# Ten staging places, another start order and a new sharing of ScalarE, VectorE and GpSimd in a fused attention and two feed-forward layers

## The chip, the cores and the metric

The kernel runs on one core of a Trainium2 chip. The metric is the device time of one execution in microseconds, as the median of the runs shown. Lower is better.

## The reference

For each of 8 batches and 8 heads, 512 tokens `x` (64 wide) attend to 32 state rows and the state rows attend to the tokens. Both results stand one behind the other as 544 rows of 512 numbers per batch (4352 rows in all). They go through a feed-forward layer with a leaky ReLU (512 to 2048 to 512) and then through a gated one (512 to 1536 to 512).

```python
scores = scale * np.matmul(x, state.transpose(0, 1, 3, 2))
a = softmax(scores);  xread = np.matmul(a, state)
scores2 = scale * np.matmul(state, x.transpose(0, 1, 3, 2))
a2 = softmax(scores2);  sread = np.matmul(a2, x)
x = concatenate([xread, sread], axis=2)     # then heads side by side
h = x @ w_in;  x = np.maximum(0.01 * h, h) @ w_out
g = x @ w_gate
out = g * sigmoid(g) * (x @ w_val) @ w_out2
```

The weights are float64 in the inputs. The kernel gets their bits as pairs of 32-bit words and rounds them to float32 itself.

## The kernel before

**Products.** A float32 operand is split into a high and a low part (`split_h` on ScalarE, line 164, `split_l` on VectorE, line 167), and a product is three TensorE passes over these parts. The first layer doesn't form `xread`: since `xread @ w_in` is `a @ (state @ w_in)`, the kernel multiplies the state by `w_in` once for all batches and then works with the softmax `a` (parts `ah`, `al`) and the product (parts `swh`, `swl`).

**The product of state and w_in.** `product_sw` (line 462) makes it for a group of 512 columns `g`, a pair of heads `p` and four batches `bs`: two matmuls, one for each head, into two PSUM banks (`ps_sw`). Both banks are copied to staging tiles `sw` (line 476) and each is stored to `sw_dram` by a transfer that SyncE issues (line 477). Head 0 of a pair has two staging tiles (pool `cv`), head 1 two others (pool `xin`), four in all. There are 32 such products, so 64 copies and 64 stores. `load_sw` (line 491) fetches a batch's rows back when that batch's turn comes. Batch 0 needs its part at once: `state_win` makes it by itself (line 456), and `keep_sw_h`, `keep_sw_l` split it out of PSUM.

**Conversion of a weight tile.** There are 32 tiles of 128 x 512 in the first layer, 16 of `w_in` and 16 of `w_out` (order: `ORDER`, line 90). A tile is loaded as `ws` (512 KB, five places), and `to_f32` (line 208) has six steps for it: `scale` (L214) and `low` (L215) on ScalarE; `sign` (L216), `limit` (L219), `join` (L222) and `add` (L225) on VectorE. `limit` caps the scaled high word, `add` adds the rounding bits of the low word to the joined word. The generator `convert` (line 234) runs them as a pipeline of four pumps to a tile: `scale` of this tile and `limit` of the one before; `low` and `sign` of this tile; `join` of the one before; `add` of the one before, with the next load, and, for `w_in`, a store to `win_dram` (L232). `w_out` tiles are then split into high and low parts (`w_parts`).

**What sets the order.** Instructions stand on each engine in the order in which the program issues them, and an engine takes them in that order. Two kinds of strings, written by hand, set it in the first stage. `START` (line 91) is walked once: `c` is one pump of the conversion, `p` one product, `0` and `1` the next step of the scores and the softmax of the first batch's two halves, `h` and `l` the high and low part of batch 0's own product, `s` and `S` the placing of the state of batch 0 and of the other batches in `states` (`place_states`, line 1223), `m` the first product with `ah`, `al` (`h_mm`, line 510). `SLOT0` (line 92) has one string for each of the 16 slots of batch 0: `c` and `p` as above, `H` the next `h_mm`, `S` and `L` its splits (`gh`, `gl`), `Y` and `Z` the halves of `y_mm`, the product with `w_out`. In `START` a product takes two of the four banks of pool `ps_y`; in `SLOT0` it takes the two single banks of `ps_a`, which the next product must find emptied. The later batches and the second layer follow, with orders of their own.

## Time and profile before

| | |
|---|---|
| median of three runs | 1471.0 us (1470.5, 1471.0, 1475.11) |
| the profiled execution's own time | 1474.11 us |
| its span, first to last instruction | 1471.8 us |
| TensorE matmuls (PE) | 1444.4 us busy, 98% of the span |
| VectorE (DVE) | 829.1 us, 56% |
| ScalarE (ACT) | 688.0 us, 47% |
| GpSimd (POOL) | 3.0 us, 8 instructions |
| DMA | 309.65 MB, mean 210 GB/s |

Busy shares are means over stages that differ. The page's 40 slices show TensorE at nine tenths or more in all slices but the first and the last. VectorE and ScalarE are busiest in the first four slices, the first 150 us, and so are the DMA engines. The chain of work that ended last is 95% TensorE. The stage to read is therefore the first one, by windows, waits and timelines.

### The profile page before, as it was taken

The page shows a single profiled execution, that of the slowest core. Times are in us where ns is not written, and L with a number is a line of the kernel's source. Part 1 is how long each engine was busy: PE and PEld are TensorE (multiplying, and loading weights), DVE is VectorE, ACT ScalarE, POOL GpSimd, SP SyncE. Part 2 cuts the span into 40 slices and gives each one's busy share as a digit, 9 for nine tenths or more (in the row PEclk, how much of TensorE's full clock was granted, in tenths as well). Part 3 has the DMA queues.
Part 4 walks back from the last instruction along what each step waited for, and adds up shares of the span by engine and source line. Part 5 has one row for each costly group of instructions (what it writes and reads, how often), then busy time and mean ns, then how long its engine had stood idle before and what let it go on. Part 6 is the DMA issues. An engine that isn't in the chain of part 4 may idle for free.

```text
span 1471.8 us, 20667 instructions
## 1 busy us (share of the span) xinstructions
PE 1444.4 (98%) x7530; PEld 1153.9 (78%) x7530; DVE 829.1 (56%) x1476; ACT 688.0 (47%) x1243; POOL 3.0 (0%) x8
## 2 busy tenths in 40 slices
PE   5999999999999999999999999999999999999998
PEld 1545777777777778888888888888888878988887
DVE  5877577676767676243454535555344655544442
ACT  6877556555656666444333433334233343333322
POOL 0000000000000000000000000000000000000000
PEclk9999999999999999999999999999999999999999
DMA  8996556665665656260668666667766397876345
GB/s 293 321 327 216 184 183 241 199 225 193 220 217 184 237 183 210 99 206 23 211 194 279 228 231 208 193 218 244 232 194 194 102 319 238 270 247 193 117 152 191
DMA packets 146788, 309.65 MB, mean 210 GB/s; under 512 B 14080, under 2 KB 34816, under 8 KB 145664
## 3 DMA queue, kind: packets, MB, share of 16 engines
q1 hardware_dynamic: 145392, 299.82, 61.8%
q10 hardware_dynamic: 1296, 8.52, 1.4%
q8 instruction: 60, 0.98, 0.3%
q14 instruction: 40, 0.33, 0.1%
HBM read 231.74 MB, written 76.55 MB: 209 GB/s over the span
## 4 chain that ended last, share of the span: by engine, by line
PE 95%; DMA 2%; ACT 1%; DVE 1%; issue 0%; SPq 0%; ACTq 0%
PE ps_y L444 24%; PE ps_o L444 18%; PE ps_x L729 18%; PE ps_h L444 14%; PE ps_s L729 9%; PE ps_a L729 4%; PE ps_t L444 2%; PE ps_sw L468 2%; PE ps_yt L444 2%; PE ps_s L319 1%; DMA sw_dram<-sw 1%; PE ps_r L416 1%; ACT sw L476 1%; DMA wo<-wo 1%; PE ps_a L402 0%
## 5 line engine op out<-in xcount | busy, mean ns | idle before, releaser
L444 PE MATMUL ps_y<-gh,w_parts 128*128 128x512 f32 x1024 | 340.5, 392 | 0.0
L729 PE MATMUL ps_x<-yc,wq 128*128 128x512 f32 x1152 | 278.1, 389 | 0.0
L729 PEld LDWEIGHTS ps_x<-yc,wq 128*128 128x128 f32 x1152 | 216.2, 188 | 44.9
L444 PE MATMUL ps_o<-wo,zh 128*128 128x512 f32 x768 | 236.4, 389 | 0.0
L444 PEld LDWEIGHTS ps_y<-gh,w_parts 128*128 128x128 f32 x1024 | 193.0, 188 | 52.1 <-issue 7.6
L444 PE MATMUL ps_y<-gl,w_parts 128*128 128x512 f32 x512 | 200.0, 391 | 0.0
L168 DVE TENSOR_TENSOR gl<-hs,gh 128x512 fp32r<-128x512 f32 (+1 forms) x144 | 95.1, 660 | 142.8 <-ACT gh L165 142.6
L444 PEld LDWEIGHTS ps_o<-wo,zh 128*128 128x128 f32 x768 | 144.1, 188 | 29.9
L537 ACT ACTIVATE hs<-ps_h 128x512 f32<-128x512 f32 (+1 forms) x144 | 82.6, 574 | 171.9 <-PE ps_h L444 168.2
L444 PE MATMUL ps_o<-wo,zl 128*128 128x512 f32 x384 | 149.5, 389 | 0.9 <-DMA wo<-wo 0.9
L729 PE MATMUL ps_s<-yc,wq 128*128 128x512 f32 x576 | 146.2, 389 | 0.0
L168 DVE TENSOR_TENSOR zl<-z,zh 128x512 fp32r<-128x512 f32 x96 | 66.3, 691 | 115.7 <-ACT zh L165 115.6
L729 PEld LDWEIGHTS ps_s<-yc,wq 128*128 128x128 f32 x576 | 108.1, 188 | 22.5
L165 ACT CAST zh<-z 128x512 fp32r<-128x512 f32 x96 | 59.3, 622 | 141.6 <-PE ps_o L444 141.5
L749 ACT ACTIVATE sg<-C 128x512 f32<-128x512 f32 x72 | 45.5, 632 | 158.2 <-DVE C L745 158.2
L444 PEld LDWEIGHTS ps_y<-gl,w_parts 128*128 128x128 f32 x512 | 96.6, 189 | 19.7
L444 PE MATMUL ps_h<-ah,swl 128*128 128x512 f32 x256 | 106.4, 416 | 1.1 <-DVE swl L168 1.1
L745 DVE TENSOR_TENSOR C<-ps_s,C 128x512 f32<-128x512 f32 x48 | 33.2, 691 | 123.0 <-PE ps_s L729 122.9
L444 PE MATMUL ps_h<-al,swh 128*128 128x512 f32 x256 | 100.4, 392 | 0.5 <-DVE al L168 0.5
L741 ACT COPY C<-ps_x 128x512 f32<-128x512 f32 x96 | 55.9, 583 | 94.7 <-PE ps_x L729 93.2
L444 PE MATMUL ps_h<-ah,swh 128*128 128x512 f32 x256 | 100.1, 391 | 0.0
L165 ACT CAST gh<-hs 128x512 fp32r<-128x512 f32 (+1 forms) x144 | 85.6, 595 | 3.0
(129 smaller groups left out, 1910.3 us busy)
## 6 DMA issues: line engine op xcount, KB each, us to landing
wo<-wo SPq DMA_DIRECT2D x96, 512.0 KB
wq<-quad_gate SPq DMA_DIRECT2D x168, 256.0 KB
wq<-quad_val SPq DMA_DIRECT2D x168, 256.0 KB
ws<-in_dram SPq DMA_DIRECT2D x68, 512.0 KB
sw_dram<-sw SPq DMA_DIRECT2D x64, 256.0 KB
sw<-sw_dram SPq DMA_DIRECT2D x56, 256.0 KB
quad_gate<-hl SPq DMA_DIRECT2D x24, 512.0 KB
quad_val<-hl SPq DMA_DIRECT2D x24, 512.0 KB
```

What stands on the lines that cost most here:

```text
L165: nc.scalar.copy(dst, src)
L168: nc.vector.tensor_tensor(out=dst, in0=src, in1=hi.bitcast(F32), op=ALU.subtract)
L319: nc.tensor.matmul(ps[2 * NS * i:2 * NS * (i + 1)], lhsT=states[:, p, b, :], rhs=xt.pop((b, p)), start=True, stop=True,)
L416: nc.tensor.matmul(ps[NS * k:NS * (k + 1), i], lhsT=v["et"][:, n:n + NS], rhs=tokens[i][:, c, NS * k:NS * (k + 1)], start=(c == 0), stop=( ...
L444: nc.tensor.matmul(ps, lhsT=w, rhs=v, start=first and n == 0, stop=last and n == len(todo) - 1)
L468: nc.tensor.matmul(ps[e], lhsT=flat[half, p, 4 * bs:4 * bs + 4, :].rearrange("d b n -> d (b n)"), rhs=raw["in", g, p][half], start=True, s ...
L476: nc.scalar.copy(t, ps[e])
L537: nc.scalar.activation(hs, ps[:, :n], AF.Prelu, alpha=0.01)
L729: nc.tensor.matmul(bank, lhsT=a, rhs=v, start=first and n == 0, stop=last and n == len(todo) - 1, skip_group_check=True,)
L741: nc.scalar.copy(t[0], src)
L745: nc.vector.tensor_tensor(out=kept[0], in0=bank, in1=kept[0], op=ALU.add)
L749: nc.scalar.activation(t[0], c, AF.Sigmoid)
```

## The change

Line numbers behind the change are those of the new file, up to 19 higher.

- The state product is staged in ten tiles, five for each head of a pair, which are taken in turn (`stage_sw`). Six of them are parts of tiles that are first used later (`yst`, `x_tail`).
- ScalarE copies the first bank of a product, VectorE the second. Of the products of batches 0 to 3 only rows 32 to 127 are stored, without batch 0's rows.
- `limit` and `add` of a first-layer tile run on GpSimd, but for the first four tiles. `add` is there an integer `tensor_tensor`. There are 28 such tiles, 56 instructions. The tiles of the second layer stay on VectorE.
- The state of batches 1 to 7 is placed by GpSimd (two copies). Batch 0's stays on ScalarE.
- ScalarE runs one copy of a 128 x 1 tile before anything else.
- `START` is another string. `SLOT0` is unchanged.

```diff
--- before.py
+++ after.py
@@ -88,7 +88,7 @@
 
     LOADS = "xswxxwww"
     ORDER = "iiiioiiooiioiioioiioioioiooooooo"
-    START = "spc0Scpccc0p0cpccpcc1ccchcc1cccpc1clcpp0hcccpclp1c01cpcmcc"
+    START = "sccccScc0ccpc0cpccp1c0cpcchc1cpcc0lp1hc0cpccpl1cpcp1cpcmcc"
     SLOT0 = [
         "DcHcpAccccSYLpcZccc",
         "DcHcAcccpSYLpccZccc",
@@ -210,19 +210,21 @@
         lo, low3 = t.bitcast(U32)[:, :, 0], t[:, :, 0]
         hi, hi_f = t[:, :, 1], t.bitcast(F32)[:, :, 1]
         v = raw[key].bitcast(I32)
+
+        engine = nc.gpsimd if key[0] in ("in", "out") and key not in keys1[:4] else nc.vector
         return {
             "scale": lambda: nc.scalar.activation(hi_f, hi_f, AF.Copy, scale=REBIAS),
             "low": lambda: nc.scalar.activation(low3, lo, AF.Copy, scale=2.0 ** -29),
             "sign": lambda: nc.vector.tensor_scalar(
                 out=v, in0=hi, scalar1=-0x80000000, scalar2=None, op0=ALU.bitwise_and
             ),
-            "limit": lambda: nc.vector.tensor_scalar(
+            "limit": lambda: engine.tensor_scalar(
                 out=hi_f, in0=hi_f, scalar1=HI_MAX, scalar2=-HI_MAX, op0=ALU.min, op1=ALU.max
             ),
             "join": lambda: nc.vector.scalar_tensor_tensor(
                 out=v, in0=hi, scalar=3, in1=v, op0=ALU.logical_shift_left, op1=ALU.bitwise_or
             ),
-            "add": lambda: nc.vector.tensor_tensor(out=v, in0=v, in1=low3, op=ALU.add),
+            "add": lambda: engine.tensor_tensor(out=v, in0=v, in1=low3, op=ALU.add),
         }
 
     ready = []
@@ -469,12 +471,25 @@
                 ps[e], lhsT=flat[half, p, 4 * bs:4 * bs + 4, :].rearrange("d b n -> d (b n)"),
                 rhs=raw["in", g, p][half], start=True, stop=True,
             )
+        staged = stage_sw()
         for e in range(2):
-
-            pool, tag, bufs = ((cv, "sw", 2), (xin, "xn", 2))[e]
-            t = pool.tile([P, 512], F32, tag=tag, name="sw", bufs=bufs)
-            nc.scalar.copy(t, ps[e])
-            nc.sync.dma_start(out=sw_dram[bs][g][2 * p + e], in_=t)
+            (nc.scalar.copy, nc.vector.tensor_copy)[e](staged[e], ps[e])
+
+            r = slice(NS, P) if bs == 0 else slice(0, P)
+            nc.sync.dma_start(out=sw_dram[bs][g][2 * p + e, r], in_=staged[e][r])
+
+    sw_stages = []
+
+    def stage_sw():
+
+        if not sw_stages:
+            y, x = ab.tile([P, KD, S], F32, tag="yst", name="sw"), first1.tile([P, 2, 512], F32, tag="x_tail", name="sw")
+            sw_stages[:] = [[y[:, 0], y[:, 1]], [y[:, 2], y[:, 3]], [x[:, 0], x[:, 1]]] + [
+                [pool.tile([P, 512], F32, tag=tag, name="sw", bufs=2) for pool, tag in ((cv, "sw"), (xin, "xn"))]
+                for _ in range(2)
+            ]
+        sw_stages.append(sw_stages.pop(0))
+        return sw_stages[-1]
 
     def sw_tiles(b, g, q):
         SW[b, g, q] = tuple(wsp.tile([P, 512], F32R, tag="ab"[q] + t, name="sw" + t) for t in "hl")
@@ -1217,13 +1232,17 @@
                 nc.sync.dma_start(
                     out=flat.rearrange("p k b n -> p (k b n)"), in_=state_t.rearrange("e d k b n -> (e d) (k b n)")
                 )
+
+        table = cv.tile([P, 1], F32, name="table")
+        nc.gpsimd.memset(table, 0.0)
+        nc.scalar.copy(table, table)
         nc.gpsimd.memset(states, 0.0)
         make_identity(nc, ident)
 
-        def place_states(some):
+        def place_states(some, copy):
             for e in range(2):
                 half = slice(D * e, D * e + D)
-                nc.scalar.copy(states[half, :, some, NS * e:NS * e + NS], flat[half, :, some])
+                copy(states[half, :, some, NS * e:NS * e + NS], flat[half, :, some])
 
         background[0] = convert(keys1, lambda key: True, place1, next_load1, (finish1_h, finish1_l))
 
@@ -1242,9 +1261,9 @@
             elif action == "l":
                 keep_sw_l(*low.pop(0))
             elif action == "s":
-                place_states(slice(0, 1))
+                place_states(slice(0, 1), nc.scalar.copy)
             elif action == "S":
-                place_states(slice(1, B))
+                place_states(slice(1, B), nc.gpsimd.tensor_copy)
             elif action in "mM":
                 f = "mM".index(action)
                 if f not in firsts:
```

Three places show what this does to the engines' order. In the rows a name is a tile, `ws` the loaded tile, `st` and `a` the softmax of a half batch, `sw` a staging tile.

VectorE, the first instructions of the program, before:

```order
L216 TENSOR_SCALAR w_in<-ws 128x512
L219 TENSOR_SCALAR ws<-ws 128x512
L333 STREAM_TRANSPOSE st<-s 128x512
L334 TENSOR_REDUCE m_189<-st 128x16
L341 TENSOR_TENSOR st<-st,m_189 128x512
L216 TENSOR_SCALAR w_in<-ws 128x512
L222 SCALAR_TENSOR_TENSOR w_in<-ws,w_in 128x512
L225 ISA w_in<-ws,w_in 128x1024
```

and now:

```order
L218 TENSOR_SCALAR w_in<-ws 128x512
L221 TENSOR_SCALAR ws<-ws 128x512
L218 TENSOR_SCALAR w_in<-ws 128x512
L224 SCALAR_TENSOR_TENSOR w_in<-ws,w_in 128x512
L227 ISA w_in<-ws,w_in 128x1024
L476 COPY sw<-ps_sw 128x512
L221 TENSOR_SCALAR ws<-ws 128x512
L335 STREAM_TRANSPOSE st<-s 128x512
L336 TENSOR_REDUCE m_216<-st 128x16
L218 TENSOR_SCALAR w_in<-ws 128x512
L476 COPY sw<-ps_sw 128x512
L224 SCALAR_TENSOR_TENSOR w_in<-ws,w_in 128x512
```

The first tile's `join` and `add` (L224, L227) have moved ahead of the softmax, and copies of the second bank stand between the steps of the conversion.

VectorE, the last instructions up to the second `al`, which the first `h_mm` needs, before:

```order
L219 TENSOR_SCALAR ws<-ws 128x512
L168 TENSOR_TENSOR swl<-ps_sw,swh 128x512
L350 TENSOR_REDUCE r_342<-st 128x16
L351 TENSOR_SCALAR r_342<-r_342 128x16
L352 RECIPROCAL r_342<-r_342 128x16
L353 TENSOR_TENSOR st<-st,r_342 128x512
L355 STREAM_TRANSPOSE a_347<-st 128x512
L216 TENSOR_SCALAR w_in<-ws 128x512
L168 TENSOR_TENSOR al<-a_300,ah 128x512
L168 TENSOR_TENSOR al<-a_347,ah 128x512
```

and now:

```order
L218 TENSOR_SCALAR w_in<-ws 128x512
L476 COPY sw<-ps_sw 128x512
L224 SCALAR_TENSOR_TENSOR raw<-ws,raw 128x512
L476 COPY sw<-ps_sw 128x512
L168 TENSOR_TENSOR swl<-ps_sw,swh 128x512
L352 TENSOR_REDUCE r_352<-st 128x16
L353 TENSOR_SCALAR r_352<-r_352 128x16
L354 RECIPROCAL r_352<-r_352 128x16
L355 TENSOR_TENSOR st<-st,r_352 128x512
L357 STREAM_TRANSPOSE a_357<-st 128x512
L218 TENSOR_SCALAR w_in<-ws 128x512
L168 TENSOR_TENSOR al<-a_357,ah 128x512
```

Two more copies stand in this piece, and the `sign` (L218) ahead of the last `al` takes a tile whose `scale` stands behind `ah<-a_357` on ScalarE.

GpSimd, behind the making of the identity, where there was nothing until the `zero` tile of a much later stage:

```order
masks.py:199 AFFINE_SELECT ident<-ident 128x128
L1245 COPY states<-flat 64x4x7x32 x2
L221 TENSOR_SCALAR ws<-ws 128x512
L227 TENSOR_TENSOR raw<-raw,ws 128x512
L221 TENSOR_SCALAR ws<-ws 128x512
L227 TENSOR_TENSOR w_in<-w_in,ws 128x512
L221 TENSOR_SCALAR ws<-ws 128x512
L227 TENSOR_TENSOR w_in<-w_in,ws 128x512
```

The pair of `limit` (L221) and `add` (L227) goes on like this for 28 tiles.

## Rows read from the trace of the kernel before

**Rows 1.** Windows: us, busy time of each engine (instructions), granted clock, DMA share, GB/s.
```profile
0.00:20.00 20.00, 7.45 (x14) 1.84 (x14) 5.93 (x11) 9.80 (x17) 2.44 (x7) 1.00 0.70 258
20.00:40.00 20.00, 16.11 (x46) 6.38 (x46) 18.83 (x38) 15.55 (x31) 0.00 (x0) 1.00 0.93 330
40.00:140.00 100.00, 93.85 (x341) 49.31 (x339) 79.95 (x151) 81.24 (x152) 0.00 (x0) 0.98 0.86 296
140.00:560.00 420.00, 420.00 (x2822) 333.20 (x2822) 293.31 (x600) 256.90 (x468) 0.53 (x1) 1.00 0.60 207
...
sum 1472.00, PE 1444.42 PEld 1153.93 DVE 829.06 ACT 687.95 POOL 2.97; mean PE 240.74 PEld 192.32 DVE 138.18 ACT 114.66 POOL 0.49
```
**Rows 2.** Waits of TensorE, 0 to 140 us: total, times, longest.
```profile
PE ps_sw L468 <- ACT sw L476: 5.3, 6, 1.5
```
**Rows 3.** Waits of ScalarE, 0 to 140 us.
```profile
ACT sw L476 <- DMA sw_dram<-sw: 4.6, 4, 1.2
ACT ws L214 <- DMA ws<-in_dram: 1.4, 3, 0.7
```
**Rows 4.** Groups by line and form, 0 to 140 us: busy us, mean ns | idle before.
```profile
L476 ACT COPY sw<-ps_sw 128x512 f32<-128x512 f32 x63 | 34.3, 590 | 13.0 <-PE ps_sw L468 7.5 <-DMA sw_dram<-sw 4.6 <-ACT hs L537 0.4
L219 DVE TENSOR_SCALAR ws<-ws 128x512 f32<-128x512 f32 x32 | 13.6, 424 | 0.0
L225 DVE CUSTOM_DVE_ANT_0 w_in<-ws,w_in 128x1024 uint16<-128x1024 uint16 x16 | 11.0, 687 | 0.2
```
**Rows 5.** The same for VectorE over the whole span: its only full-bank copy out of PSUM.
```profile
L850 DVE COPY ost<-ps_o 128x512 f32<-128x512 f32 x16 | 11.1, 691 | 27.2 <-PE ps_o L444 25.3 <-DMA wq<-quad_val 1.8
```
**Rows 6.** Timeline of GpSimd: start us, duration us.
```profile
0.73 1.80 POOL L1220 MEMSET states<- 128x2048 f32 x1 [0.29 <-POOLq L1466]
2.47 0.20 POOL masks.py:197 MEMSET ident<- 128x128 f32 x1
2.75 0.29 POOL masks.py:199 TENSOR_SCALAR_AFFINE_SELECT ident<-ident 128x128 f32<-128x128 f32 x1
```
**Rows 7.** Timeline of ScalarE at the start.
```profile
5.11 1.28 ACT L1226 ACT_TABLE_LOAD   x1 [5.11 <-DMA flat<-in_dram]
...
7.18 0.67 ACT L214 ACTIVATE ws<-ws 128x512 f32<-128x512 f32 x1 [0.17 <-DMA ws<-in_dram]
...
10.36 1.88 ACT L1226 COPY states<-flat 64x896 f32<-64x896 f32 x2
```
**Rows 8.** Timeline of TensorE (PEld its weight loads) at the start.
```profile
7.87 0.29 PEld L319 LDWEIGHTS ps_s<-xt,states 128*64 128x64 f32 x2 [0.51 <-DMA xt<-in_dram]
...
15.29 2.08 PE L468 MATMUL ps_sw<-w_in,flat 64*128 64x512 f32 x4 [5.45 <-DVE w_in L225]
17.30 1.98 PE L319 MATMUL ps_s<-xt,states 128*64 128x512 f32 x4
```
**Rows 9.** Window of 8 to 10 us, columns as in rows 1.
```profile
8.00:10.00 2.00, 1.84 (x4) 0.15 (x2) 0.73 (x2) 0.13 (x1) 0.00 (x0) 1.00 1.03 407
```
**Rows 10.** Timeline of VectorE at the start.
```profile
7.88 0.43 DVE L216 TENSOR_SCALAR w_in<-ws 128x512 int32<-128x512 int32 x1 [7.88 <-ACT ws L214]
...
20.13 0.69 DVE L225 CUSTOM_DVE_ANT_0 w_in<-ws,w_in 128x1024 uint16<-128x1024 uint16 x1
20.74 0.42 DVE L219 TENSOR_SCALAR ws<-ws 128x512 f32<-128x512 f32 x1
21.07 0.42 DVE L216 TENSOR_SCALAR w_in<-ws 128x512 int32<-128x512 int32 x1
...
36.84 0.69 DVE L168 TENSOR_TENSOR al<-a,ah 128x512 fp32r<-128x512 f32 x1 [0.79 <-ACT ah L165]
```
**Rows 11.** Timeline of TensorE in the slots of batch 0.
```profile
55.23 1.77 PE L456 MATMUL ps_sw<-w_in,states 128*64 128x512 f32 x4
...
101.94 1.13 PE L468 MATMUL ps_sw<-w_in,flat 64*128 64x512 f32 x4
103.73 1.61 PE L468 MATMUL ps_sw<-w_in,flat 64*128 64x512 f32 x4 [0.67 <-ACT sw L476]
...
113.47 1.80 PE L468 MATMUL ps_sw<-w_in,flat 64*128 64x512 f32 x4 [1.52 <-ACT sw L476]
115.20 0.79 PE L444 MATMUL ps_y<-gh,w_parts 128*128 128x512 f32 x1
```

## The prediction

> **What bounds the kernel now.** I read the windows first. From 140 to 560 us TensorE is busy in every microsecond, and over the span its busy time falls short by 27.6 us, of which 22.6 lie before 140 us: 12.55 in the first 20, 3.89 in the next 20 and 6.15 from 40 to 140 [rows 1]. The change touches this stage alone, so the question is how many of those 22.6 us it returns or adds to. What comes after is bound by TensorE and moves along unchanged. Second, the same rows show who sets the pace inside the stage. From 20 to 40 us VectorE is busy 18.83 of 20; the chain up to the first `h_mm` is VectorE's. From 40 to 140 TensorE leads with 93.85 of 100, before ScalarE (81.24) and VectorE (79.95). Third, the waits: TensorE's largest after 20 us is for ScalarE's copies of the state product, 5.3 us in 6 waits [rows 2], and ScalarE itself waited 4.6 us for stores to free a staging tile [rows 3]. Fourth, the timelines for when each of these falls.
>
> The sum goes against one execution, span 1471.8 us; it took 1474.11, the median of the runs is 1471.0, and I add the difference to the median. About 0.3% (4.4 us) is what a measurement of this kernel can tell from no change.
>
> **The change, part by part.**
>
> *Table load and placing.* ScalarE's table load (1.28 us) goes ahead of the state's arrival, and 1.88 us of copies leave ScalarE [rows 7]. The first scores still wait for their second `xt`, whose landing released TensorE at 7.87 [rows 8], and the first `scale` waits for its own load until 7.18 [rows 7]. So the load's move is worth nothing. GpSimd's copies have 896 numbers a partition. Its only rows are a memset of 2048 (1.80 us), one of 128 (0.20) and a select of 128 (0.29) [rows 6]: 0.10 us and then 0.83 to 1.52 ns a number, so 0.84 to 1.46 us each. Nobody needs these states before the first slot: nothing.
>
> *The first order.* I count VectorE's instructions up to the end of the second `al`. Long ones start 0.61 us apart and short ones (`sign`, `limit`) 0.33, as three successive rows show [rows 10]. Before: 26 long, 13 short and 4 very short (0.2 us), 21.0 us of work, between 7.88 and 37.53 us, so 8.65 us of waiting [rows 10]. Now eight copies come in, and one `add` and two `limit` go to GpSimd: 33 long and 11 short, 24.6 us. A copy out of PSUM is priced by the same copy at the kernel's end, 691 ns, as long as an `add` with 687 [rows 4, 5].
>
> Its waits, in the new order: (1) `sign` of the second tile needs that tile's load. Behind the `xt` that landed at 7.87 another `xt` and the tile are queued, 0.79 MB, at 407 GB/s [rows 9]: 9.8 us, plus a `scale` of 0.57, so 1.85 us of waiting. (2) The first copy needs the first product, which starts at about 12.0 instead of 15.29, but takes 2.08 us again [rows 8]: 2.1. (3) The copy of the third product, which itself waits for VectorE's second `add`: 1.1, if it runs like later ones (1.13 us [rows 11]), or 2.1, if like the first. (4) The next `sign` waits for a `scale` behind ScalarE's copy of the second scores (1.98 us when slow [rows 8]): 0.6 to 1.5. (5) A `sign` behind `exp`, `swh` and `scale` on ScalarE: 1.05. (6) The `sign` ahead of the last `al`, whose `scale` stands behind `ah`: 1.1. Together 7.8 to 9.7 us. So `al` ends at 7.88 + 24.6 + 7.8 to 9.7, or 40.3 to 42.2 us, 2.8 to 4.6 later than before. Eight products are done by then instead of seven, which returns 1.06 us of TensorE later. Net 1.7 to 3.6 us lost; I take **+2.7**.
>
> *Staging places and shared copies, in the slots.* (a) At 113.47 a product had waited 1.52 us and then took 1.80 instead of 1.13 [rows 11]; staging tiles not yet stored caused it. With ten places that wait ends, and next is the wait for the copy itself, some 0.7 us: −1.5. (b) Right behind that pause TensorE's matmuls are drawn out (115.20: 0.79 us [rows 11]), and the granted clock of 40 to 140 us is 0.98, so 2 us in which it was below the full 2.4 GHz [rows 1]. If the pause halves, this doesn't occur: −1.8, or 0 if a pause elsewhere brings it back. (c) Where a product follows a product, it waits 0.67 us for the first copy and is drawn out by 0.48 (1.61 against 1.13) for the second, as at 103.73 [rows 11]; there are five such places. Two engines copying at once remove the 0.48, if VectorE comes to its copy in time: 0 to −2.4, I take half, −1.2. (d) At 55.23 a `state_win` was drawn out to 1.77 [rows 11], because its tile's `add` was late; GpSimd's is later still.
>
> *Rounding steps on GpSimd.* The trace has no such operation. By the slopes above a one-input pass over 512 numbers is 0.52 to 0.88 us; for `limit` I take 0.7, in the middle. For `add` the low end is VectorE's own 0.69 [rows 4], the high end two passes by the upper slope, 1.76; I take 1.2. That is 1.9 us a tile, at 26 tiles 49 us of some 96, so GpSimd is not the pace; at the high ends it would be 69, still not. The Trainium skill (GPSIMD Engine Reference, section 3.1) gives 2.6 cycles of 1.2 GHz a number for a two-input add, an estimate of 1.1 us here; the sum by it would be the same, and no row of this trace shows it. The later `add` costs (d) 0.7 us. VectorE gets rid of 26 x 0.94 us and takes 24 copies of 0.61, ScalarE gets rid of 24 x 0.53: neither was the pace from 40 us on, so this alone gains nothing. SyncE's stores to `win_dram` and the next loads now wait for GpSimd's `add`, half the `sw` stores for VectorE, and all that is queued behind them; the five `ws` places cover it, since ScalarE waited only 1.4 us for loads in the whole stage [rows 3]. If that cover went, `scale` would wait for DMA.
>
> *Shorter stores.* 32 stores of 192 KB instead of 256 save 2.1 MB, 6 us of transfers at 330 GB/s. The engines' waits for DMA are those of [rows 3], and (a) has counted them: nothing more.
>
> **Sum.** +2.7 − 1.5 − 1.8 − 1.2 + 0.7 = −1.1 us: 1470 us, no change that can be told. Its own range is 1466 to 1475: the start at its bounds (−1.0, +0.9), (b) and (c) absent (+3.0) or (c) full (−1.2), the rest from GpSimd's bounds.
>
> **Rivals.** *GpSimd and VectorE block each other: 1479 us.* No row here has both at work. For it: GpSimd works in only 2.44 us of the first 20 and never beside a busy VectorE [rows 1, 6], so nothing excludes it, and most of VectorE's steps read two tiles. Then VectorE stands still for about half of GpSimd's 49 us. Its work from 40 to 140 us is 80 − 24.4 + 14.6 = 70 us; with 24 more it reaches 94, as much as TensorE. From 20 to 40 us, when VectorE was 94% busy, TensorE had 81% [rows 1]; it would lose up to 13 us in 100, and I take 8, with (c) lost too: 1470 + 8 + 1.2. It decides from the point where VectorE's blocked time exceeds the 26 us of slack it would have. Against it: copies out of PSUM and reductions read one tile at most, and VectorE has that slack. The Trainium skill (SBUF — State Buffer, section "Who interferes with whom") has this as a rule: VectorE's second read port is GpSimd's, held for a whole instruction, against VectorE steps with two SBUF inputs. By that rule this rival comes true at its full price; no run here shows it yet.
>
> *The early products run at full pace, and the copies are prompt: 1465.5 us.* If TensorE takes 1.13 us for each early product and as little for the scores, waits 2 to 4 shrink by some 1.9 us against my middle, and the start costs 0.8; in the slots (a), (b) and (c) return 1.5, 2.0 and 2.4, (d) costs 0.7, and ScalarE is less late elsewhere, about 1 more of the 5.3 [rows 2]: −5.4. For it: ScalarE is relieved of 13 us. Against it: the first product and the first scores ran slowly (2.08, 1.98 us [rows 8]), and pauses lie between them in the new order too.
>
> *The change does nothing:* both ends hidden, 1471 us; this is inside the forecast's range and I give it no share of its own.
>
> **How the numbers follow.** Forecast (1466 to 1475) 0.44, blocking (1473 to 1485) 0.30, prompt (1461 to 1468) 0.26. Faster by more than 4.4 us, below 1466.6: 0.20 of the last and 0.06 of the first. Slower, above 1475.4: 0.27 of the second, 0.03 of the first. The rest, 0.44, is no change. The range leaves a tenth on each side: 1463 to 1481.
>
> **What would show it.** In the changed profile: `add` of the first tile ending near 12 us and the second `al` at 40 to 42 (wrong, if at 38 or at 45); no ScalarE wait for `sw_dram`; a granted clock of 1.00 from 40 to 140; GpSimd rows of about 0.7 and 1.2 us; `join` and `gl` still at 0.69 on VectorE. If these last ones grow beside GpSimd's, blocking is right, and the time is above 1475. If products behind products show no drawn-out records and the start ends at 38, the prompt case is right.

## The result and the profile of the kernel after

The changed kernel takes 1483.35 us (median of 4 runs, 1483.06 to 1485.22), 1.0074 of the time before (95% interval 1.0061 to 1.0087; the kernel before took 1472.2 us in the four runs beside it), some 11 us longer. The forecast was 1470.0 us in a range up to 1481: it was wrong, and too low.

| | before | after |
|---|---|---|
| profiled execution, its span | 1474.11, 1471.8 us | 1485.22, 1483.4 us |
| TensorE busy | 1444.4 us | 1452.7 us |
| VectorE, ScalarE, GpSimd busy | 829.1, 688.0, 3.0 us | 835.4, 672.1, 68.0 us |
| DMA | 309.65 MB | 307.56 MB |

The windows of the kernel after answer to [rows 1], with one more from 40 to 60 us:

```profile
0.00:20.00 20.00, 8.33 (x14) 2.29 (x16) 7.13 (x13) 7.27 (x13) 4.33 (x10) 1.00 0.80 290
20.00:40.00 20.00, 16.34 (x36) 4.36 (x32) 14.38 (x26) 9.84 (x18) 1.76 (x2) 0.86 0.74 244
40.00:60.00 20.00, 16.15 (x50) 9.13 (x50) 14.07 (x24) 11.88 (x22) 8.13 (x9) 0.71 0.59 187
40.00:140.00 100.00, 88.59 (x300) 45.94 (x299) 72.39 (x113) 62.61 (x112) 51.65 (x47) 0.93 0.80 267
140.00:560.00 420.00, 420.00 (x2758) 330.57 (x2757) 301.11 (x603) 259.89 (x473) 9.72 (x9) 1.00 0.60 204
```

From 40 to 140 us TensorE went from 93.85 to 88.59, and it ran slower: the granted clock is 0.86 from 20 to 40 us and 0.71 from 40 to 60, where it was 1.00 in both. No engine stands out. VectorE fell from 79.95 to 72.39 and ScalarE from 81.24 to 62.61. Everybody waits for somebody, as the waits from 0 to 140 us tell (TensorE, then ScalarE, then VectorE):

```profile
PE ps_sw L470 <- DVE w_in L227: 6.7, 3, 3.1
...
PE ps_h L446 <- ACT ah L165: 3.0, 1, 3.0
PE ps_sw L470 <- ACT sw L476: 2.9, 5, 0.8
PE ps_sw L470 <- DVE swl L168: 2.2, 1, 2.2
...
PE ps_sw L458 <- DVE sw L476: 0.8, 1, 0.8
...
ACT sw L476 <- PE ps_sw L470: 13.3, 14, 4.6
ACT ah L165 <- DVE a L357: 11.2, 3, 5.5
...
ACT ws L216 <- DMA ws<-in_dram: 7.0, 4, 2.1
...
DVE w_in L218 <- ACT ws L216: 14.3, 7, 8.0
DVE sw L476 <- PE ps_sw L470: 12.9, 10, 2.3
```

ScalarE's wait for `sw_dram` [rows 3] is gone, and TensorE's wait for ScalarE's copies [rows 2] fell from 5.3 to 2.9 us. In their place VectorE stands 12.9 us in front of its new copies, and ScalarE 11.2 us for `a`, the last step of VectorE's softmax. VectorE's timeline in the start, with the waits in brackets:

```profile
10.63 0.43 DVE L218 TENSOR_SCALAR w_in<-ws 128x512 int32<-128x512 int32 x1 [1.70 <-ACT ws L216]
...
14.59 0.69 DVE L476 COPY sw<-ps_sw 128x512 f32<-128x512 f32 x1 [2.21 <-PE ps_sw L470]
...
21.48 0.69 DVE L476 COPY sw<-ps_sw 128x512 f32<-128x512 f32 x1 [2.27 <-PE ps_sw L470]
...
24.60 0.43 DVE L218 TENSOR_SCALAR w_in<-ws 128x512 int32<-128x512 int32 x1 [1.49 <-ACT ws L216]
...
37.11 0.43 DVE L218 TENSOR_SCALAR w_in<-ws 128x512 int32<-128x512 int32 x1 [1.13 <-ACT ws L216]
...
40.26 0.69 DVE L476 COPY sw<-ps_sw 128x512 f32<-128x512 f32 x1 [1.53 <-PE ps_sw L470]
...
45.36 0.43 DVE L218 TENSOR_SCALAR w_in<-ws 128x512 int32<-128x512 int32 x1 [1.25 <-ACT ws L216]
45.70 0.68 DVE L168 TENSOR_TENSOR al<-a,ah 128x512 fp32r<-128x512 f32 x1
```

The second `al` ends at 46.38 us; it was 37.53 before [rows 10], and 40.3 to 42.2 in the forecast. TensorE at that time:

```profile
34.33 3.66 PE L470 MATMUL ps_sw<-w_in,flat 64*128 64x512 f32 x6 [2.16 <-DVE swl L168]
38.15 2.07 PE L470 MATMUL ps_sw<-w_in,flat 64*128 64x512 f32 x2 [0.16 <-ACT sw L476]
...
44.81 0.79 PE L446 MATMUL ps_h<-ah,swl 128*128 128x512 f32 x1 [3.01 <-ACT ah L165]
46.44 0.79 PE L446 MATMUL ps_h<-al,swh 128*128 128x512 f32 x1 [0.83 <-DVE al L168]
...
47.46 0.63 PE L446 MATMUL ps_h<-ah,swl 128*128 128x512 f32 x1
47.88 0.63 PE L446 MATMUL ps_h<-al,swh 128*128 128x512 f32 x1
```

Here the passes behind `al` start 0.42 us apart. From slot 1 on they start 0.24 apart, as they did before at this place:

```profile
38.15 0.40 PE L444 MATMUL ps_h<-ah,swl 128*128 128x512 f32 x1
38.39 0.39 PE L444 MATMUL ps_h<-al,swh 128*128 128x512 f32 x1
```

The window of 44 to 46 us gives the granted clock as 0.50, the lower of its two levels (1.2 GHz). In windows of half a microsecond it was 0.91 from 34.0 to 34.5, as TensorE went on behind the pause of 2.16 us, and 0.50 right after; it was back at 1.00 from 51.5.

To see where time is lost I take from TensorE's timeline when each slot of batch 0 begins (its first pass with `ah` behind one with `gh`) and subtract the same time of before. The kernels in the lower rows are those of the next section. Each row is one execution. That of before was one of its slower ones (1474.11 us), so the last column isn't the difference of the medians: for the changed kernel the +13.0 are 11.6 us at the end of the span.

| kernel | second `al` ends | slot 1 | slot 2 | slot 8 | slot 12 and later |
|---|---|---|---|---|---|
| before | 37.53 | 48.14 | 56.93 | 109.23 | 141.75 |
| after | 46.38 | +11.2 | +12.3 | +18.1 | +13.0 |
| new order alone | 39.43 | +4.0 | +3.9 | +3.9 | +1.1 |
| ten places alone | 35.68 | −1.8 | −1.7 | −0.8 | −3.3 |
| after, ScalarE copies both banks | 40.58 | +5.0 | +6.3 | +7.6 | +2.8 |
| after, shared copies in slots only | 39.65 | +3.8 | +5.3 | +10.5 | +5.4 |
| after, VectorE copies 8 columns | 42.24 | +6.3 | +7.7 | +9.9 | +4.6 |

The loss has two places: 11 us before slot 1, and 7 more up to slot 8. Of these 5 come back, 2.8 where before had its own pause at 113 us [rows 11] and 2.3 between slots 11 and 12, where one product less is left.

### The profile page after: what moved, and what is told of

The parts are those of the page before. It is cut to its first block, busy times and chain, and to the rows that moved or that the text cites. A ratio compares the mean times of both kernels' runs of the same rounds, so it can differ in the third digit from the quotient of the medians.

```text
span 1483.4 us, 20752 instructions
## 1 busy us (share of the span) xinstructions
PE 1452.7 (98%) x7530; PEld 1156.8 (78%) x7530; DVE 835.4 (56%) x1452; ACT 672.1 (45%) x1210; POOL 68.0 (5%) x67
## 2 busy tenths in 40 slices
DMA packets 145766, 307.56 MB, mean 207 GB/s; under 512 B 14081, under 2 KB 34817, under 8 KB 144641
## 4 chain that ended last, share of the span: by engine, by line
PE 93%; DVE 2%; DMA 2%; ACT 1%; POOL 1%; issue 1%; SPq 0%; POOLq 0%; DVEq 0%; ACTq 0%
PE ps_y L446 22%; PE ps_o L446 18%; PE ps_x L744 18%; PE ps_h L446 13%; PE ps_s L744 9%; PE ps_a L744 4%; PE ps_t L446 2%; PE ps_yt L446 2%; PE ps_sw L470 2%; DMA ws<-in_dram 1%; PE ps_s L321 1%; PE ps_r L418 1%; PE ps_a L404 0%; DMA wo<-wo 0%; POOL raw L227 0%
## 5 line engine op out<-in xcount | busy, mean ns | idle before, releaser
L168 DVE TENSOR_TENSOR gl<-hs,gh 128x512 fp32r<-128x512 f32 (+1 forms) x144 | 99.0, 687 | 136.1 <-ACT gh L165 135.9
```

Source lines behind the costliest of these rows:

```text
L168: nc.vector.tensor_tensor(out=dst, in0=src, in1=hi.bitcast(F32), op=ALU.subtract)
```

## The experiments

All ratios are against the kernel before on the same chip; not all runs were on one chip. 0.1% is 1.5 us.

**1. Undo one part of the change, or do one alone.** My first theory (A) was the new order with its slow clock; the rivals were GpSimd (B) and the copies on VectorE (C).

Old `START` in the changed kernel:

```diff
-    START = "sccccScc0ccpc0cpccp1c0cpcchc1cpcc0lp1hc0cpccpl1cpcp1cpcmcc"
+    START = "spc0Scpccc0p0cpccpcc1ccchcc1cccpc1clcpp0hcccpclp1c01cpcmcc"
```

> The changed kernel with the first order of before; staging places, shared copies and GpSimd's rounding steps stay. Theory A (the new first order costs the time: the second al ends at 46.4 us instead of 37.5, and TensorE's clock is at 0.50 from about 34 to 51 us): al ends at 37 to 40, the clock is 0.9 or more from 40 to 60 us, and the time is 1473 (1470 to 1476). Theory B (GpSimd beside VectorE costs it, everywhere before 140 us): al comes back by at most 3 us, sign still takes 0.6 to 0.7 us in the slots, and the time is 1479 or more. Theory C (the copies on VectorE delay its chain): they still stand in the start, so al ends at 41 to 43 and the time is 1477 to 1480.

Measured: 1.0077 (1.0062 to 1.0092), 1483.0 us. `al` ended at 38.5 and slot 1 was only 2.1 us late, but slot 12 was 8.7 us late: what the start no longer lost went in the slots. A falls as the main cause.

No rounding on GpSimd:

```diff
-        engine = nc.gpsimd if key[0] in ("in", "out") and key not in keys1[:4] else nc.vector
+        engine = nc.vector
```

> The changed kernel with limit and add of every tile on VectorE. A: the start loses at most the 2 us by which VectorE's steps are lengthened there, al ends at 44 to 46, the clock still falls, and the time is 1480 (1478 to 1483). B: the 10 us by which VectorE's steps are lengthened and the waits for limit and add all go, al ends at 40 to 42 as forecast, time 1472 to 1475. C: VectorE has yet more to do, so nothing is gained: 1483 or more.

Measured: 1.0086 (1.0069 to 1.0103), 1484.1 us. `sign` was back at 0.42 us, and nothing was won. B falls as the main cause: taken out of the changed kernel, neither the order nor GpSimd returns anything.

Both copies of a product on ScalarE:

```diff
-            (nc.scalar.copy, nc.vector.tensor_copy)[e](staged[e], ps[e])
+            nc.scalar.copy(staged[e], ps[e])
```

> The changed kernel with both copies of a product on ScalarE. C: the eight VectorE copies of the start (8 times 0.69 us, and the waits for the products ahead of them, 2.2 us each at first) leave VectorE's chain; al ends at 38 to 41 and the time is 1474 to 1477. A: the order itself, with its products ahead of the scores, is the cause; al ends at 43 or later and the time is 1480 or more. B: as A.

Measured: 1.0019 (1.0009 to 1.0028), 1474.7 us. This one line returns 0.55%, three quarters of the loss: C.

The new `START` in the kernel before:

> The kernel before with the new first order and nothing else (four staging places, ScalarE's copies, VectorE's rounding). A: the loss is there in full, al ends at 43 to 46, the clock is at half level around 40 us, time 1479 to 1484. B: no GpSimd work, so at most 2 to 3 us are lost: 1472 to 1475. C: without copies on VectorE the order costs little: al at 38 to 40, 1472 to 1475; A is told from B and C by this run, and B from C by the two others.

Measured: 1.0022 (1.0011 to 1.0032), 1475.8 us: 3.2 us for the order.

GpSimd's rounding in the kernel before:

> The kernel before with limit and add of all but the first four tiles on GpSimd and nothing else. So far the changed kernel without GpSimd was no faster than with it. D (GpSimd gives as much as it takes: VectorE loses 0.7 us of add per tile and gets steps that are lengthened by 0.1 to 0.25 us): 1470 to 1475. B (blocking costs by itself): sign, gl and al are lengthened, the add that comes later delays TensorE, 1477 or more.

Measured: 1.0012 (1.0001 to 1.0023). `sign` took 0.70 and 0.68 us on the two kinds of tiles, `gl` 0.93; the price is 2 us, at most 3.4.

Old order, no GpSimd, shared copies and ten places:

> The changed kernel with the first order of before and with VectorE's own rounding; ten places and the shared copies stay. C (the copies on VectorE are the cause, in either order): the first product with w_out starts within 3 us of before, but TensorE falls back by 6 to 8 us up to the last slot: 1480 to 1485. A (old order, so no loss): 1472 to 1475. If GpSimd's steps, not the copies, hold the slots back in the run with the old order: 1474 to 1476.

Measured: 1.0068 (1.0047 to 1.0090), 1483.4 us. The same without shared copies:

> The kernel before with the ten staging places, the shorter stores, the earlier table load and the state placed by GpSimd, and nothing else. ScalarE's 4.6 us of waits for sw_dram go. By the prediction's terms (a) and (b) 3.3 us come back: 1467 to 1470. If ScalarE is merely late for its next step instead: 1471 to 1473.

Measured: 0.9977 (0.9966 to 0.9987), 1468.4 us, the fastest kernel of this study. Between these two only the copies differ, by 0.91%. Their windows (columns as in [rows 1]), first with shared copies, then without:

```profile
60.00:100.00 40.00, 37.10 (x125) 18.27 (x123) 34.16 (x66) 23.46 (x42) 0.00 (x0) 0.97 0.77 251
100.00:140.00 40.00, 37.47 (x140) 20.04 (x138) 35.40 (x66) 28.65 (x53) 0.00 (x0) 1.00 0.82 282
```
```profile
60.00:100.00 40.00, 35.93 (x132) 18.65 (x130) 31.75 (x61) 32.27 (x60) 0.00 (x0) 1.00 0.87 292
100.00:140.00 40.00, 37.99 (x145) 21.12 (x142) 32.05 (x61) 32.04 (x60) 0.00 (x0) 1.00 0.76 258
```

With its share VectorE is busy 69.6 of 80 us and ScalarE only 52.1; without, both have 64. The two engines were even; the shared copies made VectorE the fuller one and gave ScalarE room, and the time did not fall with it.

Shared copies in the slots alone:

```diff
-            (nc.scalar.copy, nc.vector.tensor_copy)[e](staged[e], ps[e])
+            (nc.scalar.copy, nc.scalar.copy if banks == "yy" else nc.vector.tensor_copy)[e](staged[e], ps[e])
```

> The changed kernel with both copies on ScalarE in the start and the shared copies in the slots alone. With both copies on ScalarE everywhere it took 1474.7, with all shared 1483.3. If the start has the loss (there the eight copies and their waits for a product stand in the chain to al): the second al ends at 40.6 as there, and the time is 1475 to 1477. If the slots have it: 1480 or more. By the times at which the slots begin, some 6 of the 8.6 us were lost before the second slot, so 1477 is my number.

Measured: 1.0041 (1.0027 to 1.0054). So the 0.55% are 0.22 in the slots and 0.33 in the start, each to some 0.2.

Ten places and the shorter stores alone, without the earlier table load and GpSimd's placing:

> The kernel before with the ten staging places and the shorter stores alone; the table load and the placing of the state are where they were. With these two moved as well it took 0.9977 of the time before. If the places give the gain, as the prediction's terms (a) and (b) had it: 1467 to 1470. If the relief of ScalarE by the placing (1.88 us) and the earlier table load (1.28 us) give it: 1471 to 1474.

Measured: 0.9980 (0.9970 to 0.9990): the places have the gain. ScalarE had no wait for `sw_dram` left, and the granted clock was 1.00 in every window to 160 us.

Ten places, old order, GpSimd's rounding, ScalarE's copies:

> The changed kernel with the first order of before and both copies on ScalarE: ten places and GpSimd's rounding are left of it. Ten places alone gave 0.9977, GpSimd alone 1.0012. If the parts add up: 0.9989, 1471.5 (1470 to 1473). If shared copies are the whole cause of the loss and the order costs what it cost alone (3 us), this run lies 3 us under the 1474.7 with the new order.

Measured: 1.0001 (0.9992 to 1.0011). This closes a ladder from the kernel before to the changed one, each step one part: ten places (with the table load and the placing) −0.23%, GpSimd +0.24, the order +0.18, shared copies in the slots +0.22, in the start +0.33. Its sum is the changed kernel's +0.74 because it ends there; that is no test. Each step is uncertain by 0.1 to 0.2, and the parts don't simply add: the order costs 0.18 beside ScalarE's copies and nothing (−0.03) beside the shared ones, and the shared copies cost 0.55 here and 0.91 in the old order without GpSimd.

Of GpSimd's steps `limit` alone, on the fastest kernel:

> Ten places, both copies on ScalarE, the first order of before (0.9977 so far), and of the rounding steps limit alone on GpSimd, which the join two pumps later needs; the add stays on VectorE. If GpSimd's price there (1.0001 with both steps) is the late add: VectorE wins 0.33 us a tile and this is the fastest, 1467 to 1468. If it is the lengthened steps (sign 0.42 to 0.67 us) or the join that waits for limit: 1469 to 1472.

Measured: 0.9987 (0.9977 to 0.9998). No gain. The time is that of the second case, but `sign` stayed at 0.42 us, and the difference to 0.9977 is within the noise: which part of GpSimd's share has the price isn't shown.

**2. How do VectorE's copies cost it, by their work or by the wait for the product?** First the copies' work without the wait, on the kernel with ScalarE's copies (the transposes took 0.70 us, a copy 0.69):

```diff
+        if banks == "yy":
+            nc.vector.transpose(out=dummy[:, 1], in_=dummy[:, 0])
...
```

> The changed kernel with both copies of a product on ScalarE (that alone: 1474.7, al at 40.6), and in the start one transpose of a constant tile on VectorE (0.70 us in these traces) at the place where its copy stood: the copies' work on VectorE without the wait for the product. If the work delays the chain: al at 44 or later, 1479 to 1482. If the waits do: VectorE has 12 us in which it waits there, most of it takes the work, al at 40.6 to 42, 1474 to 1477.

Measured: 1.0036 (1.0023 to 1.0049), `al` at 42.4 instead of 40.6: +0.17% for eight. The same in the slots, where there are 24 such products:

> One transpose of a constant tile on VectorE for each product of the slots, in the place of its copy, and both copies on ScalarE: the work without the wait. If the work costs the 3.5 us of the slots: 1477 to 1479. If VectorE's idle time takes it (it has 5 to 7 us of waits for gh and swh each there): 1474 to 1476.

Measured: 1.0032 (1.0021 to 1.0043): +0.13%. Then the wait without the work:

```diff
+        if banks == "yy":
+            nc.vector.tensor_copy(look[:, :1], ps[1][:, :1])
...
```

> The changed kernel with both copies of a product on ScalarE (that alone: 1474.7) and in the start, at the place of VectorE's copy, a copy of one column of the same bank: VectorE waits for the product as there, and has next to no work. VectorE's work without the wait gave 1478.6, both together 1483.3 against 1478.3 with the shared copies in the slots alone, so the start's part is 5. If wait and work add up: 1476 (1475 to 1477). If the wait is what holds the conversion and with it the next product: 1478 to 1480, al at 43 or later. If VectorE would have waited for ScalarE in the same places anyway: 1474 to 1475, al at 40.6.

Measured: 1.0061 (1.0038 to 1.0084), `al` at 47.0. And in the slots:

> The same copy of one column, but in the slots alone, beside both full copies on ScalarE. The shared copies in the slots cost 3.5 us (1478.3 against 1474.7). If VectorE's standing still in front of products (7.3 us in 8 waits there) is what costs it, swl, gl and the tiles behind come late and this run takes 1477 to 1479. If it is the work (16 copies at 0.61 us, beside GpSimd): 1474 to 1476.

Measured: 1.0071 (1.0053 to 1.0089). It looks as if the wait were everything (and there are 24 copies there, not 16), but these two runs ask another question than I meant. VectorE's waits to 145 us, of the first and of the second:

```profile
DVE look L481 <- ACT sw L476: 12.3, 7, 3.3
```
```profile
DVE look L481 <- ACT sw L476: 23.8, 17, 2.6
```

The column waited for ScalarE's copies of the same bank, not for the product, and for longer than the changed kernel waits. What they do show is that a place of VectorE's behind ScalarE is dear: 0.42 and 0.52% more than with ScalarE's copies alone. So I kept the changed kernel's own wait and took the work away:

```diff
-            (nc.scalar.copy, nc.vector.tensor_copy)[e](staged[e], ps[e])
+            (nc.scalar.copy(staged[0], ps[0]) if e == 0 else nc.vector.tensor_copy(look[:, :8], ps[1][:, :8]))
...
-            nc.sync.dma_start(out=sw_dram[bs][g][2 * p + e, r], in_=staged[e][r])
+            nc.sync.dma_start(out=sw_dram[bs][g][2 * p + e, r], in_=staged[0][r])
...
```

> The changed kernel, in which VectorE copies 8 of the 512 columns of its bank into a small tile, at the same place and after the same wait for the product, and the store of that bank sends ScalarE's tile a second time; the product of the second head of each pair is therefore left out of what follows. The two runs with a one-column copy waited for ScalarE's copies, not for the product; here the wait is the changed kernel's own, and only the work (24 times some 0.5 us) is gone. If the wait is the price: 1481 to 1484, al at 45 or later. If the work is: 1475 to 1478 (transposes of a constant in its place cost 3.9 us in the start and 2.6 in the slots), al at 41 to 43.

Measured: 1.0026 (1.0013 to 1.0039). Its wait to 145 us and, to 160 us, its group of copies:

```profile
DVE look L476 <- PE ps_sw L470: 14.0, 11, 2.2
```
```profile
L476 DVE COPY look<-ps_sw 128x8 f32<-128x8 f32 x32 | 5.2, 161 | 14.0 <-PE ps_sw L470 14.0
```

The waits stand as in the changed kernel (12.9 us there), and 0.48 of the 0.55% are gone, with `al` at 42.24. So the copies' work is most of the price and the wait for the product little of it; that the second bank's store no longer waits for VectorE in this run isn't told apart. By differences the wait costs about 0.07% and the work alone 0.30 (0.17 and 0.13), which leaves 0.18, no more than the uncertainty of such a sum. If it is real, one candidate is the bank: the transposes don't hold it and a full copy does, and TensorE's waits for VectorE's copies are 1.0 us in the changed kernel (0.8 and 0.2) against 0.2 with eight columns. No run shows this part by itself.

VectorE's copy three pumps later:

```diff
-        for e in range(2):
...
+        def empty(e):
             (nc.scalar.copy, nc.vector.tensor_copy)[e](staged[e], ps[e])
...
+        empty(0)
+        waiting[:] = [lambda: empty(1)]
```

> The changed kernel, with VectorE's copy of a product issued three pumps of the conversion later (or ahead of the next product, whichever comes first), so that VectorE does other work while the product runs. The copies' work stays. If VectorE's standing still in front of a product is what the shared copies cost (6.0 us in 3 waits ahead of the second al, 8.5 in 9 in the slots), al ends at 41 to 43 instead of 46.4 and the time is 1475 to 1479. If the work itself delays the chain to al (eight copies at 0.61 us, 4.9 us, of the 5.8 that al loses), al ends at 45 or later and the time is 1481 to 1485.

Measured: 1.0096 (1.0081 to 1.0111), the slowest of all, although VectorE's waits for products were down to 0.6 us and `al` ended at 43.2. TensorE's waits:

```profile
...
PE ps_sw L462 <- DVE swl L168: 4.5, 1, 4.5
PE ps_sw L475 <- DVE sw L482: 3.0, 6, 1.2
...
PE ps_sw L462 <- DVE sw L482: 1.0, 2, 0.7
```

VectorE's banks are emptied later, so TensorE takes over the wait: 4.0 us for these copies instead of 1.0, and 4.5 for `swl` instead of 2.2. Slot 1 began only 1.0 us earlier than in the changed kernel, so an early `al` is not enough. Neither expectation had this.

**3. The clock.** Transposes of the identity in the pauses of the start:

```diff
+        made_sw[0] += 1
+        warm({3: 10, 5: 3, 7: 6}.get(made_sw[0], 0))
...
+            passes(parts[:1], ps[:, :n], True, False)
+            warm(10)
+            passes(parts[1:], ps[:, :n], False, True)
```

> The changed kernel with 29 transposes of the identity, whose result nobody reads, in TensorE's pauses of the start: 10 ahead of the third product, 3 ahead of the fifth, 6 ahead of the seventh, 10 within the first h_mm between its two halves. They are extra work for TensorE, 0.27 us each when it runs fast. If the granted clock of 0.50 from 34 to 51 us is a price of these pauses, it stays at 1.00, the fourteen passes behind al take 0.24 us each instead of 0.43 (2.7 us), the products ahead of it take 1.13 instead of 2.08, and the time is 1476 to 1480. If the clock's fall hides behind VectorE's chain, or comes anyway: 1482 to 1485.

Measured: 1.0060 (1.0042 to 1.0078), 1481.9 us against the changed kernel's 1483.35: some 2 us, and the intervals overlap. The granted clock was 0.91 and 0.91 where the changed kernel had 0.86 and 0.71:

```profile
20.00:40.00 20.00, 15.48 (x52) 6.33 (x52) 16.91 (x32) 9.77 (x18) 2.59 (x3) 0.91 0.85 260
40.00:60.00 20.00, 17.27 (x64) 9.67 (x62) 14.87 (x25) 14.62 (x27) 9.41 (x9) 0.91 0.66 232
```

In this profile `al` ended at 43.5, slot 1 came 3.5 us earlier and slot 12 4.1. So the slow clock has a part in the loss, of 0 to 4 us; closer it isn't settled. It isn't the copies that bring it: the two windows have 0.76 and 0.90 with the new order alone, 0.78 and 0.88 with ScalarE's copies, and 0.83 and 1.00 in the fastest kernel, which has the old order. In the changed kernel it lasts longest of these. So it may be part of what the order costs, and not only of what the copies add.

## Why the prediction was wrong, by its own steps

- **Table load and placing, nothing.** Right: with and without them, 0.9977 and 0.9980.
- **First order, +2.7.** For the order by itself this was the size: +0.22% in the kernel before, +0.18 in the ladder. But the step's sum took in the eight copies, and that sum failed: `al` came 4 us after the forecast's end. From its rows, VectorE's work up to there is 26.8 us, not 24.6: steps that need the result of the step ahead of them start 0.71 to 0.74 us apart, not 0.61. The same error stood in the count of before and made its waiting 8.65 us. Its rows have only 6.85, the three below and the 0.79 of [rows 10]:

```profile
10.49 0.71 DVE L333 STREAM_TRANSPOSE st<-s 128x512 f32<-128x512 f32 x1 [1.73 <-ACT s L327]
...
13.48 0.43 DVE L216 TENSOR_SCALAR w_in<-ws 128x512 int32<-128x512 int32 x1 [0.83 <-ACT ws L214]
...
19.07 0.43 DVE L216 TENSOR_SCALAR w_in<-ws 128x512 int32<-128x512 int32 x1 [3.50 <-ACT ws L214]
```

  So the work grew by 4.0 us, near the 3.6 of the sum, and it was the waits that grew, by 4.7, where the sum had them about as before. They are 11.6, not 7.8 to 9.7: five came about as listed (1.70, 2.21, 1.49, 1.13, 1.25), the third took its upper end and a little (2.27), and one was not listed (1.53 at 40.26). Copies in the start alone: 0.33%, 4.9 us. And I ended the sum at `al`: behind it the passes ran at the lower clock, so that from `al` to slot 1 it took 12.95 us instead of 10.61.
- **Staging places (a) and the clock behind them (b), −3.3.** Right in size by themselves: −0.20 and −0.23%, 2.9 and 3.4 us. By its place the agreement is partly luck. With ten places alone the pause at 113 us shrank as forecast:

```profile
111.86 1.61 PE L468 MATMUL ps_sw<-w_in,flat 64*128 64x512 f32 x4 [0.67 <-ACT sw L474]
```

  and the clock stayed at 1.00, but this place returned 2.5 us (slots 8 to 9). Another 1.8 came ahead of slot 1, where two of ScalarE's four waits for `sw_dram` had stood (at 29 and 33 us), which the step didn't count, and 1.0 was lost between slots 6 and 7 by a longer wait for a copy (1.61 us at 98.53 instead of 0.67). In the changed kernel the clock falls elsewhere, in the start and at 100 to 108 us (0.84 and 0.74), which (b) had as its zero end and not as a loss.
- **Shared copies in the slots (c), −1.2, at most 0 on the bad side.** This step failed as much as the first, together with the sentence "neither was the pace from 40 us on, so this alone gains nothing". I set the 24 copies on VectorE against the rounding steps that it gets rid of, and priced both at nothing because its busy share was 80 of 100 us. Getting rid of the steps brought indeed nothing, but the copies cost 0.22%, 3.2 us, instead of returning 1.2. What counts is where a copy stands in VectorE's queue, as at 84 us (VectorE, then TensorE):

```profile
84.56 1.20 DVE L218 TENSOR_SCALAR w_in<-ws 128x512 int32<-128x512 int32 x1
86.30 0.69 DVE L224 SCALAR_TENSOR_TENSOR raw<-ws,raw 128x512 int32<-128x512 int32 x1 [0.54 <-POOL ws L221]
86.91 0.69 DVE L168 TENSOR_TENSOR gl<-hs,gh 128x512 fp32r<-128x512 f32 x1
87.51 0.68 DVE L476 COPY sw<-ps_sw 128x512 f32<-128x512 f32 x1
```
```profile
88.25 1.08 PE L458 MATMUL ps_sw<-w_in,states 128*64 128x512 f32 x4 [0.79 <-DVE sw L476]
```

  The product of the copy at 87.51 had ended at 85.87. The copy stood behind a lengthened `sign`, a `join` that waited for GpSimd's `limit` and a `gl`, and TensorE waited for its bank, 0.79 us. With ScalarE's copies TensorE does not wait there.
- **GpSimd, +0.7 by the later `add` (d).** The steps are a little longer than taken, 0.83 and 1.45 us instead of 0.7 and 1.2, and TensorE waited 1.5 us for GpSimd's `add` (0.8 and 0.7). The price is +0.12 and +0.24% in the two pairs of kernels with ScalarE's copies, +0.09 and −0.12 in the two with shared copies: some 2 to 4 us where VectorE has room, and nothing that can be told where it hasn't.
- **The loads, covered by five places.** They weren't: ScalarE's wait for them rose from 1.4 [rows 3] to 7.0 us. It isn't what costs the time, though: it was 7.6 us in the run with eight columns (1.0026), 5.6 in the fastest kernel and 0.9 in the run with the old order (1.0077), all to 140 us.
- **Shorter stores, nothing.** They were not run apart from the places.
- **The rival of blocking, 1479.** Of its signs `gl` is there and `join` isn't. Groups of the changed kernel, VectorE to 160 us and GpSimd over the whole span:

```profile
L168 DVE TENSOR_TENSOR gl<-hs,gh 128x512 fp32r<-128x512 f32 x14 | 13.4, 960 | 2.9 <-ACT gh L165 2.9
L224 DVE SCALAR_TENSOR_TENSOR raw<-ws,raw 128x512 int32<-128x512 int32 x16 | 11.0, 684 | 2.9 <-POOL ws L221 2.9
L218 DVE TENSOR_SCALAR raw<-ws 128x512 int32<-128x512 int32 x16 | 10.8, 672 | 1.8 <-ACT ws L216 1.8
L476 DVE COPY sw<-ps_sw 128x512 f32<-128x512 f32 x32 | 21.9, 686 | 14.6 <-PE ps_sw L470 14.5
```
```profile
L221 POOL TENSOR_SCALAR ws<-ws 128x512 f32<-128x512 f32 x28 | 23.2, 827 | 22.3 <-DVE raw L218 22.3
L227 POOL TENSOR_TENSOR raw<-raw,ws 128x512 int32<-128x512 int32 x16 | 23.3, 1454 | 35.0 <-DVE raw L224 25.9 <-ACT ws L217 5.1 <-ACT ws L216 1.7
```

  `gl` grew from 0.69 to 0.96 us, `sign` of a `w_out` tile from 0.42 to 0.67; `join` and the copies out of PSUM did not. `join` says little: it stands between a tile's `limit` and its `add`, and only one of 32 ran beside GpSimd (at 29.48 us, 0.84). Of the copies 21 of 32 did, at 0.68 to 0.70 us. All that was lengthened makes some 13 us by the groups' means, an estimate, where the rival had 24. Its time was near. Yet without GpSimd the kernel takes as long: the rival had a right mechanism of the wrong price, and its time being near proved nothing.
- **What was missing among the rivals:** the shared copies as a loss. I listed waits for them one by one and work for them in the start, but never asked what the time would be if the copies stayed where they were.

By the ladder the start (order and copies) cost 7.5 us instead of 2.7, the slots' copies 3.2 instead of −1.2, GpSimd 3.5 instead of 0.7, and (a) and (b) −3.4 as forecast. Each is uncertain by some 2 to 3 us. The first two misses are mostly one mistake: VectorE's copies were priced by mean busy shares and listed waits, and cost 8 us.

## What to carry to other kernels

A mean busy share of 80% is no room: that VectorE stood idle elsewhere did not make a new step in its queue free, and it cost where it stood ahead of something that TensorE needs. Before work is moved to relieve an engine, compare the two engines in the same window ([rows 1] already had 81 and 80 of 100 us), and take the moved steps' full length as the upper bound of their price: the eight copies of the start cost about theirs, 4.9 us of 8 x 0.61, the 24 of the slots 3.2 of 14.6, each to some 2 to 3 us. Of a change in several parts, the parts that merely give room (more staging places) can be a gain that another part hides; run them alone.

## What the runs showed of the hardware that I had not expected

- Beside GpSimd a step of VectorE with one input is lengthened too: `sign`, 0.42 us alone, had a mean of 0.67 on `w_out` tiles and 0.54 on `w_in` tiles, and took 1.20 at 84.56 us. The Trainium skill (SBUF — State Buffer, "Who interferes with whom") says that `tensor_scalar`, which `sign` is, can run in a mode that takes both ports, and that a step with at most one input in SBUF is free outside such modes; the copies out of PSUM agree with 686 ns. GpSimd pays as well: its `limit` took 0.64 us at 29.12 us, beside a copy out of PSUM for most of that time, and 0.83 in the mean.
- The first two products of the start took 3.78 us together, 1.9 each against 1.13 later, in windows whose granted clock is given as 1.00 (12 to 16 us); so did the first product of before, 2.08 us [rows 8]. In the run with transposes on VectorE the same two took 3.48 us, and the same windows gave 0.61 and 0.54. So in these runs the recorded clock of a stretch behind a long pause doesn't tell by itself how fast TensorE ran there; the rows' durations do. Why isn't shown.
